# Four more units of key-query products ahead of the recurrent chain of a DeltaNet and expert kernel

## The chip, the cores and the metric

The kernel runs as one launch on one core of a Trainium2 chip. The metric is device time in microseconds. Three runs of the kernel before took 841.39, 845.05 and 845.97 us, a median of 845.05.

## The reference, cut to what matters

The input passes three layers: a delta-rule attention with a 48 x 48 state for each of 4 x 8 heads, a mixture of eight experts with one expert per token, and a dense layer of three weight matrices and an output matrix.

```python
k_n = k / (norm(k) + 1e-06)
for t in range(768):
    kt, vt, bt = k_n[:, :, t], v[:, :, t], beta[:, :, t, None]
    y[:, :, t] = einsum('bhd,bhde->bhe', q[:, :, t], state)
    v_old      = einsum('bhde,bhd->bhe', state, kt)
    state     += bt * einsum('bhd,bhe->bhde', kt, vt - v_old)
x   = y as (3072 tokens, 384)
x   = moe(x)      # argmax of 8 gates; relu(x @ w1[e]) @ w2[e], times two gates
out = max(x @ w1, x @ w2, x @ w3) @ w_out   # elementwise maximum
```

## The kernel before, in words

The change is in the attention. Its 768 time steps are cut into 24 chunks of 32 tokens, and all 32 heads of a chunk are done together. Within a chunk the recurrence is turned into a triangular 32 x 32 system per head. Its matrix comes from the products of the chunk's keys with themselves, and its inverse T is worked out ahead of use. Six slices of four chunks each are inverted, slice by slice, on VectorE.

A **unit of products** is one call of `prods(p, j)` (lines 150 to 177): for the two chunks 2p and 2p+1 and one half j of the heads, TensorE multiplies the keys by keys and by queries (L164, 64 records in the trace), ScalarE copies the key part to G (L169) and the query part to AT (L170), and GpSimd masks AT (L147). With j = 1 ScalarE's queue also stores G in device memory (L174), from where slices 2 to 5 are read again as Z (L184), and it issues the loads of the keys and queries (KQT, L139) of chunks 2p+4 and 2p+5. There are 24 units, the list `A` in `run`; chunks 20 and 21 belong to units 20 and 21 (counted from 0), chunks 22 and 23 to units 22 and 23.

**The inverse** of a slice goes through `inv_load` (Z), `inv_n1` (on GpSimd L195 and L196), `inv_n2` (ScalarE L202 to L204, then GpSimd L206 and L207), `inv_n3` (VectorE's reciprocal L216, GpSimd L217 to L225), 30 steps on VectorE (L239 a product, L245 an addition) and `inv_end` (L252 to L254).

**The chain** runs over the 24 chunks. In a step, R is v less the state's part (L318 on TensorE, L321 on VectorE), U is T times R (L340, copied by ScalarE at L348), the new state is made from U (L360, copied to Sbd at L367), and Y, the output, comes from the state and from AT times U (L331, L377, copied to x at L381). Before the first step GpSimd scales v of chunks 0 and 1 (L308) with the result of slice 0, and nine warm-up products run on TensorE (`warm(8, ...)`, L483 and L485).

**What sets the order.** Everything is written in one fixed order by `run`. Ahead of the chain stand units 0 to NA - 1 of `A`, those from 12 on merged with the inverse steps `B[s1:]` of slice 0. The rest of the inverse steps get places in the steps of the chain by a budget per step, `put(t, f)` with t in steps. The units that are left are put at 0.05 + 0.45 k: with NA = 20 three of them go into step 0 and one into step 1. Each engine executes its instructions in that order; between engines only semaphores order them.

```python
for f in merge(B[s1:], [lambda: s.load32(0), A[11], lambda: s.inv_load(2), s.empty, lambda: s.load32(1)] + A[12:s.NA]):
    f()
s.inv_end(0)
s.warm(8, s.inv[0]["tt"])
...
for k, f in enumerate(A[s.NA:]):
    put(0.05 + k * 0.45, f)
```

Of the kernel before, what the change touches and what calls it, by code (L numbers as in the profile page):

```python
# [33 lines left out]
class Attn:  # L34
# [9 lines left out]
    def __init__(s, ctx, tc, psum, big, hp, gp, kqt, knv, bt, wgt, xd, tab, ctab, cum, ident, wrm, x2):  # L44
        s.tc, s.nc, s.psum, s.big, s.hp, s.gp = tc, tc.nc, psum, big, hp, gp
        nc = tc.nc
        s.kqt, s.knv, s.btd, s.wgtd, s.xd, s.tab, s.ctab, s.cum = kqt, knv, bt, wgt, xd, tab, ctab, cum
        s.ident, s.wrm, s.ones, s.x2 = ident, wrm, wrm[:, 0:128], x2
        s.NI = 24
        s.NP = 12  # L50
        s.NSL = 6
        s.RLB = "m"
        s.XB, s.xTs, s.RLK = 1, {}, 0
        s.CUT = 0.95
        s.NL = 4
        s.NA = 20
        s.LATE = 0.4
        s.W = (0, 1, 0)
        s.END = 13
        s.TU, s.TB, s.MF = (22.92, 22.95, 22.97), "TRT", 2  # L60

        s.BUD = (5.0, 5.6, 4.6, 5.0)

        s.ORD = {0: 0, 1: 14, 2: 36, 3: 50, 4: 66, 5: 80}
        s.prep = (2.8, 2.2, 1.5, 0.6)
        cp = s.cp = ctx.enter_context(tc.tile_pool(name="acst", bufs=1))
        s.p2 = ctx.enter_context(tc.tile_pool(name="ap2", bufs=2))
        s.dr = ctx.enter_context(tc.tile_pool(name="adr", bufs=1, space=DRAM))
        nc.scalar.preload_act_table_set("natural_log_exp_and_others")
        s.chain = False  # L70
        s.RT, s.RD, s.LT = (15.4, (15.9, 0.3), (17.4, 0.35), (21.8, 0.25)), 0.5, ((18.2, 0.45), (19.3, 0.35), (23.0, 0.05))
        s.KQT, s.AT, s.Gd, s.kv, s.TT, s.x, s.inv = {}, {}, {}, {}, {}, {}, {}
# [1198 lines left out]
```

## Time and profile before

| | |
|---|---|
| time of the runs shown | 841.39, 845.05, 845.97 us, median 845.05 |
| the profiled execution | 841.33 us, span 839.6 us |
| TensorE, matmul busy | 742.9 us, 88% of the span |
| VectorE busy | 471.0 us, 56% |
| ScalarE busy | 297.2 us, 35% |
| GpSimd busy | 228.5 us, 27% |

The shares are means over parts that differ. The attention takes about the first 270 us, the experts and the dense layer the rest. The page shows the share of each engine in 40 slices of the span; VectorE is at 9 tenths from the second slice to the seventh, TensorE from the fourteenth on. The span is what the trace covers; the time of the execution is 1.7 us longer.

### The profile page before, as it was taken

What the parts mean: (1) busy time and instruction counts of PE and PEld (TensorE: products, weight loads), DVE (VectorE), ACT (ScalarE), POOL (GpSimd) and SP (SyncE); (2) the same over time, 40 slices, a digit from 0 to 9 for tenths busy, and PEclk for the clock granted to TensorE, in tenths of its full rate; (3) what the DMA queues carried; (4) which work ended last, traced back from release to release, by engine and by line L of the source; (5) the groups of instructions that cost most, each with busy time, mean ns of one, the idle gap of its engine ahead of it and who ended that gap; (6) DMA issues with size and microseconds to landing.
All of it is one profiled execution on the core that took longest, in us unless ns stands there. A gap on an engine that the chain in (4) does not pass through costs nothing. (4 is left out here: it accounts for less than half of the span.)

```text
span 839.6 us, 20331 instructions
## 1 busy us (share of the span) xinstructions
PE 742.9 (88%) x8506; PEld 635.5 (76%) x8517; DVE 471.0 (56%) x1164; ACT 297.2 (35%) x675; POOL 228.5 (27%) x322
## 2 busy tenths in 40 slices
PE   6746877878776986999899999999999999999996
PEld 4634554555554986999899999889898898988886
DVE  3998999986544532788677795452322313233130
ACT  2213666664342331555354453222221221212111
POOL 5666456422688322034032100001001010100101
PEclk7557899999997999899899999999999999999998
DMA  8894544447634235677766697542010020000001
GB/s 218 214 218 122 144 125 121 102 126 202 169 73 140 85 77 150 235 252 221 250 207 229 235 318 269 196 185 85 10 47 29 1 76 0 29 10 10 28 1 41
DMA packets 86045, 110.28 MB, mean 131 GB/s; under 512 B 53893, under 2 KB 67148, under 8 KB 83388
## 3 DMA queue, kind: packets, MB, share of 16 engines
q1 hardware_dynamic: 57547, 87.08, 33.7%
q10 hardware_dynamic: 19360, 11.42, 5.7%
q0 software_dynamic: 9040, 10.42, 4.1%
q8 instruction: 69, 1.13, 0.6%
q14 instruction: 29, 0.23, 0.1%
HBM read 79.53 MB, written 29.36 MB: 130 GB/s over the span
## 5 line engine op out<-in xcount | busy, mean ns | idle before, releaser
L867 PE MATMUL pm<-xhm,wm 128*128 128x512 f32 x648 | 204.7, 395 | 0.0
L940 DVE TENSOR_TENSOR work<-work,pm 128x512 f32<-128x512 f32 x72 | 49.5, 688 | 175.2 <-PE pm L867 175.2
L867 PEld LDWEIGHTS pm<-xhm,wm 128*128 128x128 f32 x648 | 121.8, 188 | 29.1
L867 PE MATMUL pm<-xlm,wm 128*128 128x512 f32 x324 | 128.1, 396 | 0.0
L953 POOL DMA_INDIRECT out_dram<-work,idm x24 | 23.6, 985 | 332.3 <-ACT work L952 318.0
L840 POOL DMA_INDIRECT xg<-xd,ids x32 | 44.1, 1377 | 142.7 <-PE pt L855 122.1
L942 ACT CAST hmh<-work 128x512 fp32r<-128x512 f32 x36 | 22.4, 621 | 154.3 <-DVE work L940 154.3
L239 DVE TENSOR_TENSOR zt<-Z 128x30 f32<-128x30 f32 (+14 forms) x219 | 73.2, 373 | 3.2 <-POOL Z L218 2.6
L867 PE MATMUL pz<-wm,hmh 128*128 128x384 f32 x320 | 73.7, 334 | 0.0
L867 PEld LDWEIGHTS pm<-xlm,wm 128*128 128x128 f32 x324 | 60.9, 188 | 14.4
L245 DVE TENSOR_TENSOR Z<-Z,zt 128x30 f32<-128x30 f32 (+14 forms) x219 | 69.0, 355 | 0.0
L348 ACT COPY Ubd<-pU 32x192 f32<-32x192 f32 x148 | 45.8, 309 | 62.1 <-PE pU L340 50.2
L360 PE MATMUL pS<-Ubd,kv 128*48 128x192 f32 x368 | 42.8, 363 | 17.9 <-ACT Ubd L348 13.9
L867 PEld LDWEIGHTS pz<-wm,hmh 128*128 128x128 f32 x320 | 57.2, 188 | 0.5
L164 PE MATMUL pg<-KQT 48*32 48x64 f32 x1536 | 40.6, 291 | 18.6 <-DMA KQT<-in_kqt_dram 16.1
L164 PEld LDWEIGHTS pg<-KQT 48*32 48x32 f32 x1536 | 34.5, 151 | 25.9 <-issue 12.2
L360 PEld LDWEIGHTS pS<-Ubd,kv 128*48 128x48 f32 x368 | 22.9, 133 | 37.8 <-ACT Ubd L348 22.9
L902 ACT COPY y<-po 128x256 f32<-128x256 f32 (+6 forms) x30 | 13.3, 445 | 75.7 <-PE po L867 74.1
L367 ACT COPY Sbd<-pS 48x384 f32<-48x384 f32 x72 | 34.0, 472 | 12.0 <-PE pS L360 10.3
L859 DVE TENSOR_TENSOR xl<-pt,xh 128x256 fp32r<-128x256 f32 (+6 forms) x27 | 14.0, 520 | 42.2 <-ACT xh L858 33.2
L867 PE MATMUL pz<-wm,hml 128*128 128x384 f32 x112 | 37.4, 334 | 0.0
L891 ACT ACTIVATE hh<-ph 128x440 fp32r<-128x440 f32 (+5 forms) x48 | 23.8, 503 | 27.0 <-PE ph L867 26.5
(302 smaller groups left out, 1615.1 us busy)
## 6 DMA issues: line engine op xcount, KB each, us to landing
raw<-in_w_dram SPq DMA_DIRECT2D x12, 1536.0 KB
kv<-in_knv_dram SPq DMA_DIRECT2D x24, 384.0 KB
wd<-work SPq DMA_DIRECT2D x24, 384.0 KB
wm<-wd SPq DMA_DIRECT2D x8, 1152.0 KB
KQT<-in_kqt_dram ACTq DMA_DIRECT2D x20, 448.0 KB
xd<-x SPq DMA_DIRECT2D x24, 192.0 KB
r<-in_w_dram SPq DMA_DIRECT2D x9, 512.0 KB
raw<-x SPq DMA_DIRECT2D x6, 768.0 KB
```

The costliest lines, as they stand in the source:

```text
L164: nc.tensor.matmul(ps[b * 32:b * 32 + 32, o:o + 64], kq[:, 0, :], kq.rearrange("p k t -> p (k t)"), start=True, stop=True, tile_position=( ...
L239: nc.vector.tensor_mul(t, Z[:, a:e, m].unsqueeze(2).to_broadcast([128, e - a, n]), Z[:, m, m + 1:].unsqueeze(1).to_broadcast([128, e - a, n]))
L245: nc.vector.tensor_add(Z[:, a:e, m + 1:], Z[:, a:e, m + 1:], t)
L348: nc.scalar.copy(dst, src)
L360: nc.tensor.matmul(s.pS[q][j * 64:j * 64 + 48, g2 * 192:g2 * 192 + 192], s.kv[i][:, 0, h, :], s.Ubd[h // 4][:, h % 4, :], start=(i == 0 an ...
L367: nc.scalar.copy(dst, src)
L840: s.nc.gpsimd.indirect_dma_start(t[0:r.ct], None, s.xd[0:2049] if k < 2 else s.xd, bass.IndirectOffsetOnAxis(s.gid[k][0:r.ct, c, 0:1], 0))
L867: s.nc.tensor.matmul(ps, a, b, start=(start and k == 0), stop=(stop and k == n - 1))
L891: nc.scalar.activation(hi, ps, AF.Relu)
L940: nc.vector.tensor_max(m, m, ps)
L942: nc.scalar.copy(hi, m)
L953: nc.gpsimd.indirect_dma_start(s.out, bass.IndirectOffsetOnAxis(i[:, c, 2:3], 0), y, None, bounds_check=3071, oob_is_err=False)
```

## The change

One number changes. `NA`, the number of units that stand ahead of the chain, becomes 24, so `A[s.NA:]` is empty and no unit stands in steps 0 and 1.

```diff
-        s.NA = 20
+        s.NA = 24
```

No instruction is added or removed, and the orders of VectorE and SyncE stay as they were. On TensorE, where the chain starts, units 20 and 21 stood after the warm-up products, before and behind the first U (pU); unit 22 stood behind pY and unit 23 behind the U of step 1. Before:

```order
L485 MATMUL pwarm<-wrm 128x512
L164 MATMUL pg_0_1313<-KQT_1019 32x64 x16
L164 MATMUL pg_0_1313<-KQT_1116 32x64 x16
L340 MATMUL pU_0_1367<-kv_767,T_1229 32x48 x16
L340 MATMUL pU_0_1368<-kv_767,T_1229 32x48 x16
L164 MATMUL pg_1_1415<-KQT_1019 32x64 x16
L164 MATMUL pg_1_1415<-KQT_1116 32x64 x16
L485 LDWEIGHTS wrm
L485 MATMUL pwarm<-wrm 128x512
L360 MATMUL pS_160<-Ubd_156,kv_767 48x192 x4
```

After, the four units follow the twentieth one (unit 19, here pg_1_1150) directly (KQT_1098 holds chunks 21 to 23), and the warm-up products with the rest of the chain stand behind them:

```order
L164 MATMUL pg_1_1150<-KQT_1007 32x64 x32
L164 MATMUL pg_0_1197<-KQT_1007 32x64 x16
L164 MATMUL pg_0_1197<-KQT_1098 32x64 x16
L164 MATMUL pg_1_1239<-KQT_1007 32x64 x16
L164 MATMUL pg_1_1239<-KQT_1098 32x64 x16
L164 MATMUL pg_0_1283<-KQT_1098 32x64 x32
L164 MATMUL pg_1_1325<-KQT_1098 32x64 x32
L483 MATMUL pwarm<-ttb_1362,ident 128x32
L485 LDWEIGHTS wrm
L485 MATMUL pwarm<-wrm 128x512
```

All the units that had stood among the chain have moved in front of its pwarm, and pU follows the last pwarm.

On GpSimd, the masks of the four units stood behind L195 and L196 of slice 3 and further back; between the masks of the units in front and the preparation of slice 2 there was only the scaling of v:

```order
L147 TENSOR_TENSOR AT_1036<-AT_1036,maskA 128x8x32 x2
L147 TENSOR_TENSOR AT_1125<-AT_1125,maskA 128x8x32 x2
L308 TENSOR_TENSOR kv_767<-kv_767,n_1227 128x384
L308 TENSOR_TENSOR kv_843<-kv_843,n_1227 128x384
L195 TENSOR_SCALAR vss_1245<-Z_821 128x32
L196 AFFINE_SELECT Z_821<-Z_821 128x1024
L206 TENSOR_SCALAR vt_1248<-vt_1248 128x32
L207 TENSOR_TENSOR vt_1248<-vt_1248,vss_1245 128x32
```

Now the masks of units 20 to 23 (AT_1196 and AT_1282) stand ahead of the scaling of v and of L195 to L207 of slice 2:

```order
L147 TENSOR_TENSOR AT_1018<-AT_1018,maskA 128x8x32 x2
L147 TENSOR_TENSOR AT_1107<-AT_1107,maskA 128x8x32 x2
L147 TENSOR_TENSOR AT_1196<-AT_1196,maskA 128x8x32 x2
L147 TENSOR_TENSOR AT_1282<-AT_1282,maskA 128x8x32 x2
L308 TENSOR_TENSOR kv_761<-kv_761,n_1376 128x384
L308 TENSOR_TENSOR kv_831<-kv_831,n_1376 128x384
L195 TENSOR_SCALAR vss_1394<-Z_815 128x32
L196 AFFINE_SELECT Z_815<-Z_815 128x1024
L206 TENSOR_SCALAR vt_1397<-vt_1397 128x32
L207 TENSOR_TENSOR vt_1397<-vt_1397,vss_1394 128x32
```

ScalarE's order changes in the same way: the eight copies of the four units and the two stores of G now stand behind the last two loads of KQT and ahead of L202 to L204 of slice 2, where four of the copies used to stand about the copies of the first U and four in steps 0 and 1.

## Rows read from the trace of the kernel before

**Rows 1.** Busy time by stretch: us, PE (x), PEld, DVE, ACT, POOL, PEclk, DMA, GB/s.

```profile
40.00:80.00 40.00, 22.89 (x710) 17.02 (x715) 37.30 (x115) 10.85 (x36) 26.29 (x38) 0.63 0.76 194
...
110.00:120.00 10.00, 7.02 (x198) 5.03 (x197) 9.79 (x31) 6.50 (x20) 5.81 (x10) 1.00 0.36 109
```

**Rows 2.** Timeline of VectorE at the chain's start: start us, us, instruction, [idle before].

```profile
63.08 2.04 DVE L270 STREAM_TRANSPOSE T<-ttb 128x1024 f32<-128x1024 f32 x1
...
70.83 0.35 DVE L216 RECIPROCAL vt<-vt 128x32 f32<-128x32 f32 x1
...
73.97 0.19 DVE L239 TENSOR_TENSOR zt<-Z 128x30 f32<-128x30 f32 x1 [2.60 <-POOL Z L218]
...
78.44 1.53 DVE L245 TENSOR_TENSOR Z<-Z,zt 128x108 f32<-128x108 f32 x2
...
80.72 1.64 DVE L239 TENSOR_TENSOR zt<-Z 128x58 f32<-128x58 f32 x2
82.28 0.45 DVE L245 TENSOR_TENSOR Z<-Z,zt 128x58 f32<-128x58 f32 x2
82.65 0.54 DVE L321 TENSOR_TENSOR R<-kv,pR 128x384 f32<-128x384 f32 x1
...
92.51 0.56 DVE L321 TENSOR_TENSOR R<-kv,pR 128x384 f32<-128x384 f32 x1 [0.32 <-POOL vt L222]
```

**Rows 3.** Timeline of GpSimd, same columns.

```profile
60.20 0.72 POOL L147 TENSOR_TENSOR AT<-AT,maskA 128x256 f32<-128x256 f32 x1 [1.14 <-ACT AT L170]
63.24 1.62 POOL L308 TENSOR_TENSOR kv<-kv,n 128x384 f32<-128x384 f32 x2 [2.32 <-DVE n L268]
...
66.92 0.34 POOL L207 TENSOR_TENSOR vt<-vt,vss 128x32 f32<-128x32 f32 x1
...
76.69 0.34 POOL L195 TENSOR_SCALAR vss<-Z 128x32 f32<-128x32 f32 x1
...
78.36 1.46 POOL L147 TENSOR_TENSOR AT<-AT,maskA 128x256 f32<-128x256 f32 x2
...
80.63 0.75 POOL L147 TENSOR_TENSOR AT<-AT,maskA 128x256 f32<-128x256 f32 x1 [0.16 <-ACT AT L170]
```

**Rows 4.** Timeline of TensorE, same columns; a unit of products is 64 records of L164.

```profile
56.12 1.10 PE L164 MATMUL pg<-KQT 48*32 48x64 f32 x46 [0.24 <-DMA KQT<-in_kqt_dram]
57.79 1.65 PE L164 MATMUL pg<-KQT 48*32 48x64 f32 x50 [0.57 <-issue]
...
64.01 3.10 PE L485 MATMUL pwarm<-wrm 128*128 128x512 bf16 x7 [0.22 <-issue]
67.17 1.10 PE L164 MATMUL pg<-KQT 48*32 48x64 f32 x64
...
83.25 1.50 PE L340 MATMUL pU<-R,T 32*32 32x48 f32 x64 [1.55 <-DVE R L321]
84.68 1.93 PE L164 MATMUL pg<-KQT 48*32 48x64 f32 x64
...
93.15 0.88 PE L340 MATMUL pU<-R,T 32*32 32x48 f32 x64
```

**Rows 5.** Timeline of ScalarE, same columns; ACTq is its queue of DMA issues.

```profile
60.30 2.79 ACTq L139 DMA_DIRECT2D KQT<-in_kqt_dram  x2
...
77.07 0.23 ACT L202 ACTIVATE vn<-vss 128x32 f32<-128x32 f32 x1 [4.97 <-POOL vss L195]
```

**Rows 6.** DMA by queue, 55.2 to 57.3 us, then 63.2 to 67: packets, MB, share.

```profile
q10 hardware_dynamic: 1931, 0.28, 84.7%
...
q10 hardware_dynamic: 285, 0.90, 85.2%
```

**Rows 7.** Busy time in stretches of 2 us, columns as in the first group.

```profile
56.00:58.00 2.00, 1.31 (x55) 1.07 (x59) 2.00 (x6) 0.65 (x2) 2.00 (x2) 0.50 0.91 116
...
68.00:70.00 2.00, 2.00 (x148) 1.78 (x136) 1.97 (x12) 1.64 (x6) 0.00 (x0) 1.00 0.85 326
...
78.00:80.00 2.00, 1.31 (x28) 0.97 (x32) 2.00 (x4) 1.93 (x6) 2.00 (x4) 0.50 0.00 0
```

## Prediction

> **What bounds the kernel now.** I began with the busy time by stretch of the span [rows 1]. From 40 to 80 us, where the change is made, VectorE is busy for 37.3 of 40 us, and it stays so while the chain runs (9.8 of 10 us from 110 us on). TensorE is far from full there, at a granted clock of 0.63. So a microsecond counts in this stretch only if VectorE loses or gains it, or if the chain of steps becomes later than VectorE.
>
> Next, VectorE in order of time around the start of the chain [rows 2]. It finishes the inverse of slice 0 and turns T (63.08 to 65.12), works at the inverse of slice 1, reaches the reciprocal of slice 2 (L216) at 70.83, and soon idles 2.60 us for GpSimd's multiplication L218. The first R that needs a state (82.65) stands behind inverse steps in its order, as nearly all later ones do. GpSimd over the same stretch [rows 3] shows what L216 waits for: the mask of the twentieth unit (unit 19) ends at 60.92, the two scalings of v start at 63.24, L207 ends at 67.26. VectorE came to L216 3.6 us after that: this is the slack of the path.
>
> Then TensorE [rows 4]. The products run when their K and Q have landed: the last unit and a half in front of the chain start at 56.12 after a wait for KQT and end at 59.44. The four other units lie among the chain, the first at 67.17, the last at 84.68 between the products of step 1. ScalarE [rows 5] issues the loads of chunks 22 and 23 at 60.30, 2.79 us for both, and it waits 4.97 us until 77.07 for GpSimd before it can copy the first state to SBUF. That wait is what ends step 0, and no product delays it.
>
> Last, the DMA traffic [rows 6]. Between 63.2 and 67 us ScalarE's queue (q10) moves 0.90 MB; the two loads are 448 KB each, 0.92 MB. So chunks 22 and 23 have only just been read when the chain starts, and in the kernel before nothing waits for them.
>
> **The change part by part.** No instruction is added or taken away, and the orders of VectorE and SyncE stay the same. Four units move, each with 64 matmul records, two ScalarE copies and a GpSimd mask, and with them two stores of G. TensorE, ScalarE and GpSimd execute in order, so all that stood behind the twentieth unit now waits for chunk 23: on TensorE the warm-up products and the first U; on ScalarE the activations L202 to L204 of slice 2 and the copies of U; on GpSimd the scalings of v and L195, L196, L206 and L207 of slice 2. The stores of G are queued behind the last loads and delay none of them.
>
> 1. Landing of chunk 23. With 0.02 MB to go at 67.0, its data end at about 67.1 [rows 6]. For chunk 19, the small packets of a G store already fill the queue from 55.2 [rows 6], and TensorE came off its wait at 56.12 [rows 4], about 1.0 us later. I take 68.1. The bounds are 67.1 (no delay) and 69.1 (twice that).
>
> 2. From landing to the last mask. The same run of work was done for chunk 19: the wait ends at 56.12, half a unit and a unit until 59.44 [rows 4], the copies, the mask until 60.92 [rows 3], so 4.80 us and an end at 72.9. It holds at TensorE's lower level, 1.2 GHz, which the profile grants in that stretch (0.50 [rows 7]). At the full clock a unit takes 1.10 us (67.17 [rows 4]), and one and a half 1.65, which with the 3.32 us from 56.12 to 59.44 is 1.7 us less. The waits for KQT that went with 0.50 stay, and the warm-up products after which it was 1.00 [rows 7] now come behind the units, so I take the lower level.
>
> 3. From the last mask to L216. The scalings of v start at 63.24 and L207 ends at 67.26 [rows 3], 4.02 us with nothing but ScalarE's three activations between. So L207 ends at 76.9, and VectorE, done with its steps at 70.8 as before, stands until then: 76.9 - 70.83 = 6.1 us. The chain's first U is no issue: T has been ready since 65.12, TensorE's warm-up products (seven take 3.10 us [rows 4]) end by about 75.5, and the copies of U follow; but the first state still waits for GpSimd's L195 of slice 3 (76.69 [rows 3]), which comes after L216 and L218 and so is 6.1 us later too.
>
> 4. What comes back. The masks no longer run beside the inverse steps of steps 0 and 1. Two masks at 78.36 lie beside a pair of VectorE additions that took 1.53 us, where a pair with little beside it took 0.45 (82.28): 1.05 us. One at 80.63, and a scaling behind it, lie beside a pair of 1.64: 1.15 us, half of it the mask's, 0.55 [rows 2, 3]. The fourth mask I price like the third. Together 2.2 us. Where the masks move to, VectorE either waits anyway or has its wait for L216 to absorb the collision. TensorE and ScalarE gain about 1.9 us (84.68 [rows 4]) and two copies in step 1, but the R of step 2 stands behind VectorE's work; as VectorE had been free 0.32 us before that R (92.51 [rows 2]), 0.3 us of its lateness is absorbed. The bounds of the return are 1.0 (the first two masks alone) and 3.3 (each mask in full, with the 0.3).
>
> The Trainium skill's page "SBUF — State Buffer", section "SBUF: two separate sides", has VectorE instructions with two SBUF inputs and GpSimd instructions that read SBUF exclude each other for whole instructions. By it the four masks would give back their full durations, 1.46 + 0.75 + 0.75 = 3.0 us [rows 3], and the sum would be 2.8 us. The rows agree that they collide, and give 2.2.
>
> Sum: 6.1 - 2.2 - 0.3 = +3.6 us. From there VectorE has almost no idle time for long (9.79 of 10 us from 110 us on [rows 1]) and the chain goes on step by step into the experts, so I let it pass to the end undiminished. The extremes: landing at 67.1, full clock and 3.3 back give 6.1 - 1.0 - 1.7 - 3.3 = +0.1; landing at 69.1, 1.0 back and one more stall like the 0.57 us ahead of 57.79 [rows 4] give 6.1 + 1.0 + 0.57 - 1.0 = +6.7. The profiled execution took 841.33 us with a span of 839.6, so it would take 844.9. The median of the runs shown, 845.05, is 3.7 above it; the same 3.6 us on the median give 848.6.
>
> **Rivals.** Nothing is given back. In step 1 TensorE lacks the unit that helped to keep it busy, stays at the lower level a step longer, and R is late for VectorE too. U takes 1.50 us at the lower level (83.25) and 0.88 at the higher (93.15) [rows 4]; with R and Y, each about as many records, a step costs some 1.9 us more, which eats what the masks give. It decides if TensorE is still at 0.50 when R of step 2 is computed. For it: the clock is 0.50 at 78 to 80 us in the kernel before [rows 7]. Against: U, X, a warm-up product and the state products still follow each other there. Time 845.05 + 6.1 = 851.2, and 853.1 with a second such step.
>
> The chain is better off. The loads land in time, and steps 0 and 1 become shorter by the masks, and by the last unit on TensorE. It decides if L207 ends before 70.83, so if chunk 23 lands 6.1 us earlier, near 62.0. For it: the queue has only these two loads and one G store to move after 60 us. Against: the load itself is being issued until 63.09 [rows 5]. In full 2.2 + 1.9 = 4.1 us, 840.9.
>
> Part of the wait is hidden: landing at 67.1, full clock. That is the lower extreme, 845.2, no change.
>
> **How the numbers follow.** A measurement of this kernel can tell about 0.5%, 4.2 us, from no change. The main case (1.5 to 5 us) has 0.55; most of it is inside that bound, but near its edge, so a fifth of it, 0.11, counts as slower. Nothing given back has 0.28, all slower. The partly hidden wait has 0.10, no change. The better chain has 0.07, of which 0.05 counts as faster. So slower 0.39, faster 0.05, same 0.56. The range runs from the lower extreme less 1.2 us for the scatter of the runs, 844, to the first rival with a second slow step, 853.
>
> **What would show it.** TensorE's last wait for KQT ends near 68 and its last unit near 71.4, with the clock at 0.50; GpSimd's last mask ends near 73; VectorE idles about 6 us before L216 at 77, and again 2.6 us after it; ScalarE's wait for L195 of slice 3 ends near 83.2; R of step 1 comes near 87, R of step 2 near 96, and the rest is shifted as a whole. If the wait ends near 64, or L216 comes near 71, terms 1 to 3 are wrong. If L216 is late but the R's of steps 3 to 6 are not, the chain had slack that I did not see.

## The result and the profile after

The change is slower. Over 20 runs each the median is 849.16 us against 841.67, and the ratio of the runs is 1.0068 with a 95% interval of 1.0046 to 1.0090, which is +5.7 us (3.9 to 7.6). The two medians lie 7.5 us apart; two runs of the change (856.28 and 856.54 us) were in a slower state, the ratio leaves them out, and without them the medians are 6.7 us apart. The forecast was +3.6 us, called no change by a narrow margin; the time lies inside its range. The median of the three runs that were shown before, 845.05, was 3.4 us above the median of twenty, so the forecast of 848.6 lies nearer to 849.16 than its difference deserves. The profiled execution of the changed kernel took 851.29 us, span 849.6.

VectorE over the start of the chain, kernel after (start us, us, instruction, [idle before]); it answers to [rows 2]:

```profile
63.55 2.07 DVE L270 STREAM_TRANSPOSE T<-ttb 128x1024 f32<-128x1024 f32 x1
...
70.40 0.43 DVE L245 TENSOR_TENSOR Z<-Z,zt 128x99 f32<-128x99 f32 x2
80.09 0.35 DVE L216 RECIPROCAL vt<-vt 128x32 f32<-128x32 f32 x1 [9.26 <-POOL vt L207]
...
87.69 0.47 DVE L245 TENSOR_TENSOR Z<-Z,zt 128x108 f32<-128x108 f32 x2
...
90.29 0.54 DVE L321 TENSOR_TENSOR R<-kv,pR 128x384 f32<-128x384 f32 x1
...
99.22 0.54 DVE L321 TENSOR_TENSOR R<-kv,pR 128x384 f32<-128x384 f32 x1
```

VectorE finishes T within half a microsecond of before and its steps at 70.8, as before. Then it idles 9.26 us for L207; in the kernel before L216 started at 70.83 without a wait. The pair of additions beside which the masks used to lie takes 0.47 us (87.69) instead of 1.53. R of step 1 is 7.64 us later than before, R of step 2 6.71 us.

GpSimd, kernel after, which answers to [rows 3]:

```profile
75.50 0.72 POOL L147 TENSOR_TENSOR AT<-AT,maskA 128x256 f32<-128x256 f32 x1 [0.58 <-ACT AT L170]
76.17 1.61 POOL L308 TENSOR_TENSOR kv<-kv,n 128x384 f32<-128x384 f32 x2
...
79.80 0.25 POOL L207 TENSOR_TENSOR vt<-vt,vss 128x32 f32<-128x32 f32 x1
...
85.95 0.34 POOL L195 TENSOR_SCALAR vss<-Z 128x32 f32<-128x32 f32 x1
```

The last mask (75.50) now stands right ahead of the scalings of v, and L207 ends at 80.05. L195 of slice 3, on which the first state waits, is at 85.95 instead of 76.69.

TensorE, kernel after, which answers to [rows 4]:

```profile
57.20 1.10 PE L164 MATMUL pg<-KQT 48*32 48x64 f32 x46 [0.30 <-DMA KQT<-in_kqt_dram]
58.91 1.65 PE L164 MATMUL pg<-KQT 48*32 48x64 f32 x50 [0.61 <-issue]
...
67.65 1.08 PE L164 MATMUL pg<-KQT 48*32 48x64 f32 x32 [1.29 <-DMA KQT<-in_kqt_dram]
72.32 2.39 PE L164 MATMUL pg<-KQT 48*32 48x64 f32 x96 [3.59 <-DMA KQT<-in_kqt_dram]
...
78.48 0.88 PE L340 MATMUL pU<-kv,T 32*32 32x48 f32 x64
```

Unit 19 ends at 60.56, 1.1 us later than before. Unit 22 starts at 67.65 with chunk 22, and its second half and unit 23 wait until 72.32 for chunk 23; the first U is at 78.48. The busy time in a stretch of 2 us (columns as in [rows 1]) shows that the last units ran at the lower clock level, 0.50, as forecast:

```profile
72.00:74.00 2.00, 1.68 (x80) 1.68 (x84) 0.00 (x0) 0.54 (x2) 0.00 (x0) 0.50 0.33 58
```

ScalarE, kernel after, which answers to [rows 5]; ACTq is its queue of DMA issues:

```profile
61.43 2.55 ACTq L139 DMA_DIRECT2D KQT<-in_kqt_dram  x2
...
66.66 0.38 ACT L170 COPY AT<-pg 128x256 f32<-128x256 f32 x1
69.79 0.39 ACTq L174 DMA_DIRECT2D gd<-Gd  x1
...
78.22 0.23 ACT L202 ACTIVATE vn<-vss 128x32 f32<-128x32 f32 x1 [2.80 <-POOL vss L195]
...
86.32 0.23 ACT L202 ACTIVATE vn<-vss 128x32 f32<-128x32 f32 x1 [4.67 <-POOL vss L195]
```

The last loads are issued at 61.43, about 1 us later than before. The store of G of units 20 and 21 has its data at 66.8, when the copy to G ends, and is issued only at 69.79. L202 of slice 2 starts at 78.22, and that of slice 3 at 86.32, 9.25 us later than before.

DMA by queue, kernel after, 66 to 68 us and then 68 to 70 us (packets, MB, share); q10 is ScalarE's queue, q1 SyncE's:

```profile
q1 hardware_dynamic: 113, 0.46, 72.1%
q10 hardware_dynamic: 61, 0.18, 30.3%
...
q10 hardware_dynamic: 87, 0.34, 59.4%
q1 hardware_dynamic: 89, 0.24, 40.9%
```

The kernel before moved the two loads ahead of anything of q1 [rows 6]. Here q1's 0.9 MB (Z of slice 3, k and v of chunk 2) begin at 66 us beside them, and the second load has its data near 70 us instead of 67.

From R of step 2 to R of step 15 the chain is 6.4 to 7.1 us late. In steps 16 to 22 the difference is between 5.4 and 12.5 us, at R of step 23 it is 5.9, and the last output of the dense layer leaves TensorE's banks (L952) 5.8 us late, 838.8 against 833.0. The profiled execution has 4.1 us more at its very end: in the chain that ended last, two of the last scattered stores of the output took 4.58 and 4.34 us where the kernel before had 2.59. Nothing in the program leads from the change to there, and the ratio of the runs gives +5.7, not +10.

### The profile page after: what moved, and what is told of

The parts are those of the page before. It is cut to its first block, busy times and chain, and to the rows that moved or that the text cites. A ratio compares the mean times of both kernels' runs of the same rounds, so it can differ in the third digit from the quotient of the medians.

```text
span 849.6 us, 20339 instructions
## 1 busy us (share of the span) xinstructions
PE 742.5 (87%) x8504; PEld 636.6 (75%) x8517; DVE 476.2 (56%) x1164; ACT 298.1 (35%) x675; POOL 226.0 (27%) x322
## 5 line engine op out<-in xcount | busy, mean ns | idle before, releaser
L239 DVE TENSOR_TENSOR zt<-Z 128x30 f32<-128x30 f32 (+14 forms) x219 | 74.9, 381 | 3.2 <-POOL Z L218 2.6
L164 PE MATMUL pg<-KQT 48*32 48x64 f32 x1536 | 43.5, 304 | 25.6 <-DMA KQT<-in_kqt_dram 21.9
L245 DVE TENSOR_TENSOR Z<-Z,zt 128x30 f32<-128x30 f32 (+14 forms) x219 | 63.6, 330 | 0.0
L164 PEld LDWEIGHTS pg<-KQT 48*32 48x32 f32 x1536 | 36.6, 158 | 33.2 <-issue 11.8
L360 PE MATMUL pS<-Ubd,kv 128*48 128x192 f32 x368 | 42.2, 360 | 21.8 <-ACT Ubd L348 14.6
L360 PEld LDWEIGHTS pS<-Ubd,kv 128*48 128x48 f32 x368 | 22.0, 132 | 41.7 <-ACT Ubd L348 24.7
```

Of the source, the lines that this page charges most:

```text
L164: nc.tensor.matmul(ps[b * 32:b * 32 + 32, o:o + 64], kq[:, 0, :], kq.rearrange("p k t -> p (k t)"), start=True, stop=True, tile_position=( ...
L239: nc.vector.tensor_mul(t, Z[:, a:e, m].unsqueeze(2).to_broadcast([128, e - a, n]), Z[:, m, m + 1:].unsqueeze(1).to_broadcast([128, e - a, n]))
L245: nc.vector.tensor_add(Z[:, a:e, m + 1:], Z[:, a:e, m + 1:], t)
L360: nc.tensor.matmul(s.pS[q][j * 64:j * 64 + 48, g2 * 192:g2 * 192 + 192], s.kv[i][:, 0, h, :], s.Ubd[h // 4][:, h % 4, :], start=(i == 0 an ...
```

## The experiments

Twelve runs follow: ten edited kernels, and the change itself twice more. Ratios are to the kernel before on the same chip, with 95% intervals. In the kernels with late masks one line was added, so their line numbers are one higher (L217 is the reciprocal L216, L322 is R, L321).

**Two units instead of four.** Units 22 and 23 stay in step 0.

```diff
-        s.NA = 24
+        s.NA = 22
```

> NA = 22: units 20 and 21 in front, units 22 and 23 in step 0 as units 20 and 21 were before (unit 22 still stands ahead of the first U on TensorE, behind the warm-up products). Theory A (what costs is that GpSimd's scalings and preparation of slice 2, and ScalarE's L202, stand behind the copies and masks of the units that wait for chunk 23): the first U still waits for chunk 23, until about 73, but L216 comes at 71 to 72.5, R of step 1 at 82 to 84, and the time is 0 to 2 us above before (841.7 to 843.7). Theory B (each unit in front costs its share, by TensorE's time at the lower clock level and by its copies): half of the measured 5.7 us, 844.5. Theory C (the chain is late because TensorE waits for chunk 23 ahead of the first U): as after, 847 and more.

The ratio is 1.0008 (0.9976 to 1.0041), median 841.06. TensorE and VectorE in this kernel:

```profile
71.85 1.56 PE L340 MATMUL pU<-kv,T 32*32 32x48 f32 x64
```

```profile
73.06 0.34 DVE L216 RECIPROCAL vt<-vt 128x32 f32<-128x32 f32 x1
...
84.34 0.54 DVE L321 TENSOR_TENSOR R<-kv,pR 128x384 f32<-128x384 f32 x1
...
93.27 0.54 DVE L321 TENSOR_TENSOR R<-kv,pR 128x384 f32<-128x384 f32 x1
```

The first U is late here as well (71.85 against 68.19 before), but L216 is at 73.06, without a wait ahead of it and 2.2 us later than before, and R of step 2 (93.27) is only 0.8 us late. So a first U 3.7 us late costs nothing that can be measured, and two units of four cost nothing that can be told from zero. C is out. B's price, 844.5, is a ratio of 1.0035 and lies inside the interval; what speaks against B is the 0.8 us. A holds, with L216 and R of step 1 (84.34) a little beyond its bounds.

**Three units.**

```diff
-        s.NA = 24
+        s.NA = 23
```

> NA = 23: unit 22 in front as well; its second half needs chunk 23, so its mask stands ahead of slice 2's preparation. Theory A: L216 at 78 to 79.5, about 1.5 us sooner than after (one unit, its copies and its mask less), R of step 1 near 89.5, time 4 to 5 us above before (846 to 847): nearly the whole loss comes between NA = 22 and 23. Theory B: three quarters of the loss, 846, with NA = 22 at 844.5. Theory C: as NA = 22.

The ratio is 1.0039 (1.0003 to 1.0074). VectorE:

```profile
74.90 0.35 DVE L216 RECIPROCAL vt<-vt 128x32 f32<-128x32 f32 x1 [4.94 <-POOL vt L207]
```

A wait of 4.94 us appears with the third unit. The ratio is 3.3 us, more than half of the loss, but its interval (0.3 to 6.2 us) leaves that open. L216 came sooner than I expected (78 to 79.5), since chunk 23 had landed at 66.53 in this execution. The copies of unit 22 did not follow at once: TensorE ended that unit at 67.61, and ScalarE's copy started at 69.57, behind the store of G at 69.14. About 2 us of this wait are that store's; what it waits for is told at the third execution of the change.

**No wait for chunks 22 and 23.** Units 22 and 23 read the keys and queries of chunks 20 and 21.

```diff
-                    kq = s.KQT[2 * p + st][j * 64:j * 64 + 48, b, g]
+                    kq = s.KQT[2 * p + st - (2 if p == 11 else 0)][j * 64:j * 64 + 48, b, g]
```

> The change with units 22 and 23 computed from the keys and queries of chunks 20 and 21 instead of 22 and 23 (this leaves the products of chunks 22 and 23 wrong; the loads and all orders stay): no unit in front waits for chunk 22 or 23. Theory A: units 22 and 23 follow unit 21 at once, two times 2.1 us at the lower clock level, so TensorE's last unit ends near 70.6 instead of 74.7, L216 comes near 76 instead of 80.1, and the time is 3 to 4 us below after (845). So some 5 us of VectorE's wait are left, which is the units' own work. Theory B' (the landing of chunk 23 does not matter, the units' place does): as after, 849.

The ratio is 1.0057 (1.0021 to 1.0092). TensorE and VectorE:

```profile
62.27 3.02 PE L164 MATMUL pg<-KQT 48*32 48x64 f32 x127 [0.51 <-issue]
68.44 1.70 PE L164 MATMUL pg<-KQT 48*32 48x64 f32 x52 [3.14 <-issue]
```

```profile
75.73 0.35 DVE L216 RECIPROCAL vt<-vt 128x32 f32<-128x32 f32 x1 [5.65 <-POOL vt L207]
```

L216 is at 75.73, as theory A said (76), but the gain in time is smaller than the 3 to 4 us expected: 0.9 us against the change, inside the intervals. TensorE did not run through: it stands 3.14 us at "issue" inside unit 23, and ends it at 70.14. ScalarE's copies of unit 22 stood behind the store of G, issued at 69.30, and started at 69.73. So even with no wait for chunk 22 or 23, VectorE loses 4.9 us. How much of that is the units' own work is not shown, since these two holds are in it; the late landing costs only the part above it.

**The other queue's loads out of the way.** Z of slice 3 and k and v of chunk 2 are issued from ScalarE's queue, behind the loads of KQT.

```diff
-            nc.sync.dma_start(z, s.gd[sl].rearrange("a b c i k -> (a b c) i k"))
+            (nc.scalar if sl == 3 else nc.sync).dma_start(z, s.gd[sl].rearrange("a b c i k -> (a b c) i k"))
...
-        s.nc.sync.dma_start(s.kv[i], s.knv[i])
+        (s.nc.scalar if i == 2 else s.nc.sync).dma_start(s.kv[i], s.knv[i])
```

> The change with the loads of Z of slice 3 and of k and v of chunk 2 issued from ScalarE's queue, behind the loads of KQT, instead of SyncE's. Theory D (chunk 23 lands at 72.3 and not at 68.1 because 0.9 MB of SyncE's queue are moved at the same time): the wait for KQT ends at 68.5 to 70, L216 at 76.5 to 78, and the time is 2 to 3.5 us below after (846). Theory E (it is late for its own sake, by its issue or by the G store of units 18 and 19 ahead of it): the wait ends at 71.5 or later, time as after.

The ratio is 1.0053 (1.0022 to 1.0083). TensorE and VectorE:

```profile
65.97 2.31 PE L164 MATMUL pg<-KQT 48*32 48x64 f32 x76 [1.25 <-DMA KQT<-in_kqt_dram]
68.80 1.71 PE L164 MATMUL pg<-KQT 48*32 48x64 f32 x52 [0.52 <-issue]
```

```profile
75.85 0.35 DVE L216 RECIPROCAL vt<-vt 128x32 f32<-128x32 f32 x1 [6.68 <-POOL vt L207]
...
86.07 0.54 DVE L321 TENSOR_TENSOR R<-kv,pR 128x384 f32<-128x384 f32 x1
...
95.00 0.54 DVE L321 TENSOR_TENSOR R<-kv,pR 128x384 f32<-128x384 f32 x1
```

There is no second wait for KQT to be seen: chunk 23 had landed by about 67.1, when the first half of unit 22 was done. L216 is at 75.85, sooner even than D had it (76.5 to 78), and the wait at "issue" is 0.52 us. This execution is the one that the prediction described: it had 76.9, 87 and 96 for L216 and the two R's, with a landing one microsecond later. One profile does not settle D, since chunk 23 landed at 66.5 to 67.7 in some executions with those loads in place (below). The edit also took Z's load from ahead of the store of G, which was then issued at once (65.15). The time falls less than expected: +4.5 us against +5.7, a difference that the intervals do not separate.

**Late masks with the change.** The masks of units 20 to 23 run in steps 13 and 14.

```diff
-        s.mask(p, j)
+        if p < 10:
+            s.mask(p, j)
...
+        for k, (p, j) in enumerate([(p, j) for p in range(10, NP) for j in range(2)]):
+            put(13.05 + k * 0.45, lambda p=p, j=j: s.mask(p, j))
```

> The change (NA = 24) with the masks of units 20 to 23 moved from GpSimd's place ahead of the scaling of v to steps 13 and 14, where VectorE has room. GpSimd's scaling of v and L195 of slice 2 no longer stand behind them; ScalarE's L202 still stands behind the copies of unit 23. Theory A: L308 starts at 63 to 64 as in the kernel before, and L216 comes 0.7 us for the mask, 1.6 for L308 and some 1 us for L195 and L196 sooner than it would after the same landing: 4.2 to 4.6 us after TensorE's last unit has ended became 1.5 to 2. Time 2.5 to 3.5 us below after (846), not as before, since ScalarE still waits. Theory F (GpSimd's masks alone are the wait): L216 near 71, time as before or below.

The ratio is 1.0031 (0.9998 to 1.0064), 3.1 us below the change, as expected, though the two intervals overlap. VectorE:

```profile
74.19 0.35 DVE L217 RECIPROCAL vt<-vt 128x32 f32<-128x32 f32 x1 [3.65 <-POOL vt L208]
```

TensorE's last unit ended at 72.15, and L216 follows it by 2.04 us, where it followed by 5.34 to 5.38 us in the three profiles of the change, in the one with the other queue's loads moved and in the one with the G store moved (below). The rest of the wait is ScalarE's L202 (here L203) behind the copies. A holds and F is out.

**Late masks alone, in the kernel before.** The same edit with NA = 20.

> The kernel before (NA = 20) with only the masks of units 20 to 23 moved to steps 13 and 14. This prices the part that the change gives back. Theory A (the masks cost VectorE 2.2 us in steps 0 and 1, and VectorE is the bound there): the pairs of additions beside L147 fall from 1.53 and 1.64 us to 0.5 and 1.1, R of step 1 comes 1.6 us and R of step 2 about 2 us sooner, and the time is 1.5 to 2.5 us below before (839.5). Rival: the chain's own work bounds those steps, and the time is as before.

The ratio is 0.9980 (0.9958 to 1.0003). VectorE:

```profile
71.52 0.34 DVE L217 RECIPROCAL vt<-vt 128x32 f32<-128x32 f32 x1
...
81.73 0.54 DVE L322 TENSOR_TENSOR R<-kv,pR 128x384 f32<-128x384 f32 x1
...
91.32 0.56 DVE L322 TENSOR_TENSOR R<-kv,pR 128x384 f32<-128x384 f32 x1 [0.62 <-POOL vn L225]
```

From L216, R of step 1 comes after 10.21 us, against 11.82 before [rows 2] and 10.20 with the change. So the masks cost 1.6 us up to there, and 1.9 us up to R of step 2 (19.80 against 21.68). The time agrees with A (1.7 us less), but its interval reaches zero.

**Ten late masks, in the kernel before.** As the last one with the masks of units 14 to 23 (p from 7 on) in steps 13 to 16, 0.3 of a step apart.

> The kernel before (NA = 20) with the masks of units 14 to 23 moved to steps 13 to 16. In front of the chain, masks lie beside VectorE additions of 3.17, 1.08, 1.62 and 1.04 us where pairs without one take 0.5 to 0.6. Theory A (VectorE bounds from 20 to 180 us): slice 0 is done 3 to 5 us sooner (T near 59), R of step 1 is 4 to 6 us sooner, time 4 to 6 us below before (836.5). Rival: the products' loads bound the front (unit 19 ends at 59.5, then the warm-up products and the first U), so no more than 2 to 3 us come of it (839).

The ratio is 0.9949 (0.9927 to 0.9971), 4.3 us below the kernel before: the best of all. VectorE:

```profile
59.08 2.05 DVE L271 STREAM_TRANSPOSE T<-ttb 128x1024 f32<-128x1024 f32 x1
...
77.06 0.54 DVE L322 TENSOR_TENSOR R<-kv,pR 128x384 f32<-128x384 f32 x1
...
85.98 0.54 DVE L322 TENSOR_TENSOR R<-kv,pR 128x384 f32<-128x384 f32 x1
```

T is ready 4.0 us sooner, R of step 1 5.6 us and R of step 2 6.5 us, as A had it or more. The gain in time (2.4 to 6.1 us) speaks for A rather than for the rival's 2 to 3.

**Ten late masks and two units fewer in front.** NA = 18.

> As the last one with NA = 18: units 18 to 23 in steps 0 to 2, masks of units 14 to 23 in steps 13 to 16, so that the chain's start waits for chunk 17 alone. If the loads bound the front once VectorE is relieved, this is 1 to 3 us below the last one (835); if not, it is the same or, by the six units on TensorE and ScalarE in steps 0 to 2, up to 2 us above it.

The ratio is 1.0028 (1.0001 to 1.0054), 6.6 us above the last one, where I had expected 3 below to 2 above. VectorE:

```profile
100.76 0.56 DVE L322 TENSOR_TENSOR R<-kv,pR 128x384 f32<-128x384 f32 x1 [4.39 <-issue]
```

Step 1 starts as in the last run, but VectorE has nothing left 4.39 us ahead of R of step 3; TensorE had stood 2.75 us at "issue" inside the U of step 2 (92.68). So moving units the other way, into the chain, costs as well.

**The preparation of slice 2 ahead of unit 20, masks late, NA = 24.**

```diff
-        for f in merge(B[s1:], [lambda: s.load32(0), A[11], lambda: s.inv_load(2), s.empty, lambda: s.load32(1)] + A[12:s.NA]):
+        for f in merge(B[s1:], [lambda: s.load32(0), A[11], lambda: s.inv_load(2), s.empty, lambda: s.load32(1)] + A[12:20] + [lambda: (s.inv_n1(2), s.inv_n2(2))] + A[20:s.NA]):
...
-                        elif sl == 2 and g != s.inv_load:
+                        elif sl == 2 and g == s.inv_n3:
```

> The change (NA = 24) with both things that it put behind units 20 to 23 taken from there again: the masks of these units run in steps 13 and 14, and the first part of slice 2's preparation (L195, L196, L202 to L204, L206, L207) stands ahead of unit 20 on GpSimd and ScalarE. TensorE's order is the change's, so the first U still waits for chunk 23. Theory A (VectorE's wait for L216 is the loss): VectorE idles under 0.5 us ahead of L216, which comes near 71, and the time is 1 to 3 us below before by the masks, as with NA = 20 and the masks late (839.8), plus up to 2 us if the first state, some 6 us after the first U at 74 to 78, becomes what R of step 1 waits for. Theory C (TensorE's late first U is the loss): 846 or more.

The ratio is 1.0025 (0.9989 to 1.0061). VectorE:

```profile
70.32 0.35 DVE L217 RECIPROCAL vt<-vt 128x32 f32<-128x32 f32 x1
...
84.61 0.56 DVE L322 TENSOR_TENSOR R<-kv,pR 128x384 f32<-128x384 f32 x1 [4.70 <-PE pR L319]
```

The wait ahead of L216 is gone (70.32), as A has it, and another has come in its place: R of step 1 waits 4.70 us for the state's products, as chunk 23 landed at 71.52 and the first U stood at 77.83. I had expected a time below the kernel before; the interval (0.9 us less to 5.1 more) does not show one. R of step 1 is 2.0 us late, as the expectation allowed. C has a part once A's wait is taken away.

**The change twice more.** Two more profiles, of one execution each.

> The change once more, for one more profile. If the landing of chunk 23 differs from execution to execution with what the other queue moves beside it, the wait for KQT of unit 22's second half ends anywhere from 67 to 72.3 us, and L216 follows it by 7.5 to 8 us: 75 to 80. If 72.3 is fixed by the program, it is 72.3 again.

> The change a third time, as the run before it and with the same expectation.

The first took 849.83 us: chunk 23 landed at 71.82 and L216 was at 79.59. The second took 844.10 us; its TensorE and VectorE:

```profile
67.71 1.09 PE L164 MATMUL pg<-KQT 48*32 48x64 f32 x44 [0.23 <-DMA KQT<-in_kqt_dram]
70.02 1.70 PE L164 MATMUL pg<-KQT 48*32 48x64 f32 x52 [1.21 <-issue]
```

```profile
77.08 0.35 DVE L216 RECIPROCAL vt<-vt 128x32 f32<-128x32 f32 x1 [6.97 <-POOL vt L207]
...
87.29 0.54 DVE L321 TENSOR_TENSOR R<-kv,pR 128x384 f32<-128x384 f32 x1
...
96.21 0.54 DVE L321 TENSOR_TENSOR R<-kv,pR 128x384 f32<-128x384 f32 x1
```

Chunk 23 landed at 67.71 here, and L216, R of step 1 and R of step 2 are at 77.1, 87.3 and 96.2. So the landing differs by 4.6 us from execution to execution of the same program. L216 follows it by 9.37 us, and not by 7.5 to 8 as expected. Two holds lie in between, and both can be named. ScalarE in this execution, then DMA by queue from 66 to 68 us:

```profile
70.32 0.39 ACTq L174 DMA_DIRECT2D gd<-Gd  x1
70.75 0.37 ACT L169 COPY Gd<-pg 128x256 f32<-128x256 f32 x1 [5.36 <-DMA Z<-gd]
...
q10 hardware_dynamic: 34, 0.09, 14.6%
q8 instruction: 1, 0.02, 3.4%
```

The store of G waits for the landing of SyncE's load of Z of slice 3: the profile names it, and in the semaphore records of the trace the store's wait is for the semaphore that this load updates, with the last update at 70.24 and the end of the wait at 70.28 (69.72 and 69.75 in the first profile of the change). The two lie within 0.05 us of each other in all eight profiles in which the store's data were there before Z. This is a wait of the program, and ScalarE's copies of unit 22 stand behind it.

The pause of TensorE follows the queue q8, whose packets the profile calls "instruction". Its packet of 16 KB lasts here from 67.59 to 68.67, and TensorE goes on 1.35 us later (70.02). In all profiles of this document every pause of more than 0.2 us at "issue" inside the products of L164, L340 and L360 between 30 and 110 us ends 1.2 to 1.7 us after such a packet. So these pauses look like waits for instructions; no run tested it. With a late landing the packet comes while TensorE waits for chunk 23 anyway (69.32 to 70.50 in the first profile), and units 22 and 23 run without a pause.

**The G store behind unit 23.** In the third execution the copies of unit 22 stood behind ScalarE's store of G, held until 70.32. Here both stores follow unit 23.

```diff
-            if sl > 1:
-                a = p % 2 * 2
-                nc.scalar.dma_start(s.gd[sl][a:a + 2].rearrange("s h b i k -> (b i) (s h) k"), G.rearrange("p s h k -> p (s h) k"))
+            if sl > 1 and p != 10:
+                for a in ((0, 2) if p == 11 else (p % 2 * 2,)):
+                    nc.scalar.dma_start(s.gd[sl][a:a + 2].rearrange("s h b i k -> (b i) (s h) k"), s.Gd[sl][:, a:a + 2].rearrange("p s h k -> p (s h) k"))
```

> The change with the G store of units 20 and 21 issued behind the copies of unit 23, beside the store of units 22 and 23, instead of between units 21 and 22. In the profiles of the change ScalarE is held 2.2 to 5.3 us at the issue of that store (68.6 to 70.3 instead of 65.0 to 67.0), and the copies of unit 22 stand behind it. Theory H (that hold is a part of the loss where chunk 23 lands early, near 67.7): the copies of unit 22 follow TensorE at once, and with an early landing L216 comes 8.0 to 8.8 us after it (75.7 to 76.5) instead of 9.4 (77.08 in the third run of the change); with a late landing, near 72, L216 comes 7.5 to 8 us after it as before; median time 0.5 to 1.5 us below that of the change, 1.0055 times before. Theory H0 (no part): 9.4 us after an early landing again, and the ratio of the change, 1.0068.

The ratio is 1.0062 (1.0027 to 1.0098). TensorE:

```profile
67.35 1.09 PE L164 MATMUL pg<-KQT 48*32 48x64 f32 x44 [0.31 <-DMA KQT<-in_kqt_dram]
69.88 1.71 PE L164 MATMUL pg<-KQT 48*32 48x64 f32 x52 [1.44 <-issue]
```

The copies of unit 22 followed at once (68.50), yet unit 23 ended at 71.59 for a wait of 1.44 us at "issue", and L216 came at 76.94, 9.6 us after the landing. H is not borne out: the hold at the store lies beside TensorE's own pause, which again ends 1.45 us after a packet of q8 (67.36 to 68.43). Chunk 23 landed early, so the run says nothing on the store with a late landing.

## Why the prediction was right in its mechanism and short in its size

**The mechanism was right, place by place.** The loss is VectorE's wait at L216 for GpSimd's L207, behind the masks of units that wait for chunk 23. From the end of unit 23 on TensorE to L216 the terms of steps 2 and 3 give 5.50 us; the change's executions show 5.38 (74.71 to 80.09) and 5.36 (71.72 to 77.08). The pieces were shown one by one: with the masks late only 2.0 of it are left, with the preparation in front L216 does not wait at all, and with NA = 22 no loss can be told from zero.

**The return was right.** I priced it at 2.2 + 0.3 us. From L216 to R of step 2 the kernel before needs 21.68 us and the change 19.13, so 2.55 us came back; 1.62 of it up to R of step 1, where I had 1.6. The late masks alone gave 1.6 and 1.9. The two pairs of additions differ from the quiet one by 1.08 and 1.19 us, where I wrote 1.05 and 1.15; it changes nothing. The rule that the prediction took from the Trainium skill's page "SBUF — State Buffer", section "SBUF: two separate sides", by which the masks would give back 3.0 us, was further off.

**Term 1 failed in size.** I took the landing of chunk 23 as 68.1 with bounds of 67.1 and 69.1, as in the kernel before, where the two loads had q10 to themselves. The profiles of the change have 72.32, 71.82 and 67.71. In the late ones the loads were issued 0.5 to 1.1 us later (60.80 and 61.43 against 60.30), their data were still on their way when Z and kv began on q1 near 66 us, and the two queues shared the engines until 70 us: 0.52 MB of q10 and 0.70 MB of q1 in 4 us in the first profile. What separates late from early is how much was left then. When q1's first packet moved, 0.53, 0.51 and 0.78 MB of the two loads were left (by the packets of q10 over 1 KB) in the three late profiles, the first two of the change and the one with the preparation in front, where chunk 23 landed at 71.5 to 72.3. It was 0.06 to 0.12 MB in the kernel before and in the seven other profiles in which q1's loads start behind them, where it landed at 66.5 to 68.6. With those loads moved away chunk 23 had landed by about 67.1. I had seen q1's 0.9 MB start right behind the loads and treated that order as given; nothing in the program makes it so. The Trainium skill's page "DMA: Bandwidth & Descriptors", section "Queues, rings and completion order", says that each DMA engine takes turns between the queues that have work, and the trace of 66 to 70 us agrees; had I weighed it, the late landing would have been a bound.

**Term 2 was an average, and a path was missing.** From the landing to the end of the last mask I took 4.80 us. It is 3.90 with the late landing of the first profile, where TensorE does not pause, and 5.49 with the early one, where it stands 1.21 us at "issue". So the third execution comes near the forecast of 76.9 partly by luck: it landed 0.4 us earlier and ran 0.7 us longer. The prediction said that the stores of G delay none of the loads, and it did not see that such a store waits for Z's landing, and that ScalarE's copies of unit 22 wait behind it, until 70.75 in the third execution and until 69.73 where no unit waits for chunk 23.

**Lost over gained.** With the landing of 67.71, R of step 2 is 3.7 us late (96.21), and with 72.32 it is 6.7; the three profiled executions of the change and the one with its G store moved (6.7, 6.2, 3.7 and 3.6) have a mean of about 5 us. Up to the end single executions differ by more than that: the last L952 is 5.8, 7.9, 2.7 and 7.3 us late in the four. The ratio of the runs gives +5.7. So the forecast described the better executions of the change at R of step 2, and the measured +5.7 lies beyond the 4.2 us that it called no change, though its interval (3.9 to 7.6) begins below it. How many of the runs had a late landing is not known.

**Rivals.** That nothing is given back is refuted by the 2.55 us, although its time (+6.1) was nearer; its condition, TensorE's lower clock, was not met either: the granted clock was 1.00 from 94 to 98 us, where R of step 2 is made. That the chain is better off failed on the landing, as the prediction said.

**Open.** Two things about the late landing were not tested. No run sets how much of the loads is left when q1's data start, so that this rests on comparing profiles. And in the three late profiles the last of the load's sixteen landing marks comes 1.1 to 1.2 us behind the fifteenth; what holds that one back, a 16 KB packet of q8 (1.18 us in the first profile) or the small packets of the G store behind it in q10, was not separated.

## What to carry to other kernels

Work that is moved ahead of a chain into idle time puts everything that follows it in the in-order engines behind its last input. Look which engine is the bound there, and which of its inputs comes from an engine that now waits: it was a mask of 0.7 us, needed 20 steps later, and the copies ahead of it that held back the preparation of VectorE's next slice. The cheaper move was the other one: leave the products, and put off the small operations that collide with the bound engine (ten masks late, 0.9949).

## What had not been expected of the hardware

A load that is done at 67 us when its queue is alone landed at 71.5 to 72.3 us where 0.9 MB of another queue started while more than half of the last two loads was still to be moved, and which of the two happens differs between executions of the same program. TensorE's pauses at "issue" inside small products, 0.2 to 3.1 us long, end 1.2 to 1.7 us after a 16 KB packet of the instruction queue. Masks on GpSimd beside VectorE's back-to-back steps cost both sides: taking ten of them away from the front brought T 4.0 us sooner, and of the 24 masks of the kernel before, with a median of 0.73 us, the longest took 4.4 us there.
